# Chunked attention and a feed-forward block on one core: transposes of one pair of token blocks on VectorE, statistics of one tile on ScalarE, and another order of the first tile's steps

## The chip, the core and the metric

The kernel runs on one core of one Trainium2 chip. The metric is the device time of one execution in microseconds. A core has TensorE (PE, with its weight loads shown as PEld), VectorE (DVE), ScalarE (ACT), GpSimd (POOL) and SyncE (SP, which here only issues copies). Each takes its own instructions in program order and waits for others by semaphores.

## The reference, cut to what matters

Attention within chunks of 64 tokens, then a layer norm and a feed-forward block with a residual. There are 8 batches x 576 tokens = 4608 tokens, 8 heads of 64, so 512 features, and 2048 hidden units, all float32.

```python
scores = scale * np.matmul(q_c, k_c.transpose(0, 1, 2, 4, 3))
scores = scores - np.max(scores, axis=-1, keepdims=True)
attn = np.exp(scores)
attn = attn / (np.sum(attn, axis=-1, keepdims=True) + 1e-09)
out = np.matmul(attn, v_c)
...
mu = np.mean(x, axis=-1, keepdims=True)
var = np.mean((x - mu) ** 2, axis=-1, keepdims=True)
xn = (x - mu) / np.sqrt(var + 1e-06) * g_ln
ch = np.maximum(xn @ w_ch1, 0.0) @ w_ch2
return (x + ch).astype(np.float32)
```

## The kernel before, in words

**Tiling.** 256 tokens are a pair, two pairs are a tile of 512 tokens, and there are nine tiles. A tile goes through attention pair by pair and then through the feed-forward block, whose 2048 hidden units are 16 blocks f of 128. Every product of the block is made of three products of rounded numbers: each operand is kept as a high half and a low half (`xth` and `xtl` for the tokens, `hh` and `hl` for the hidden units, two halves in `wp` for the weights), and high x high, high x low and low x high are added up. `up` (L437) makes h of one f, `split` (L447 on ScalarE, L448 on VectorE) rectifies it and splits it into `hh` and `hl`, `down` (L459) adds its share to y. After f = 15, `root` makes 1/sqrt(var + 1e-6), the power on GpSimd (L469), and `finish` (L475) adds the residual.

**Attention of a pair**, as a generator that stops at each `yield`: load q and k; scores into PSUM bank s (L243); maximum `top` (L250) and load of v; subtract it and exponentiate; transpose the probabilities; divide by their sum `den` while the value products (L327) are read out; statistics `mv` by `bn_stats` (L371); the scaled and centred tokens `xg` (L376); their transpose and its split into `xth` and `xtl`. In tile 0 and tile 1 the transposes are done by TensorE (L287, L390), and the low half by a product that subtracts the high half in PSUM (L397, the correction). From tile 2 on VectorE transposes blocks of 32x32 (L298, L410), ScalarE makes the high half (L415) and GpSimd the low half (L416).

**The weights** come as 64-bit floats, and are turned into float32 halves on the chip in 17 units: unit 0 and unit 1 are the two halves of f = 0 (512 KB each), unit i from 2 on is f = i - 1 (1 MB). For each unit SyncE copies it (L105), ScalarE takes the magnitude (L121), VectorE rounds and joins the words (L128, L129, L132) and sets the sign (L139), ScalarE makes the high half (L145). The low half is made by TensorE for units 0 and 1 (L158, L159), for units 2 to 10 by a copy of GpSimd's queue that adds to what ScalarE left there (L147, L162), and for the rest by VectorE (L164).

**The order** of all this is written by hand as strings, one letter for one step of one generator: `START` until tile 0 is through, `STEADY` for each tile in between, `LAST` for the last. a and b are the attention of pairs 0 and 1, A and B that of pairs 2 and 3, E that of the next tile's first pair; w is a step of the weights; u, v, y and 1, 2, 3 are the products and the splits of tile 0 (pair 0 alone, pair 1 alone, both); k is two spare products (L195), whose result nothing reads.

Of the kernel before, what the change touches and what calls it, by code (L numbers as in the profile page):

```python
# [8 lines left out]
F32 = mybir.dt.float32  # L9
# [48 lines left out]
def chunk_attention_ffn(ctx: ExitStack, tc: tile.TileContext, qkv, v01, g, w, out):  # L58
    nc = tc.nc
# [4 lines left out]
    work = ctx.enter_context(tc.tile_pool(name="work", bufs=2))  # L64
# [3 lines left out]
    small = ctx.enter_context(tc.tile_pool(name="small", bufs=4))  # L68
# [134 lines left out]
            ys[pair] = [ps_y.tile([P, DM], F32, name="y") for _ in range(2)]  # L203
        return ys[pair]

    def attention(pair, xt_cols, xs, by_pe, den_by_pe):

        if pair == 1:
            qk = const.tile([P, 2, HP, PAIR], F32, name="qk_b", tag=f"w{NF - 4}")
# [156 lines left out]


        mv = small.tile([P, 2, 2], F32, name="mv", bufs=6)
        for j in range(2):
            stats = small.tile([P, nc.vector.BN_STATS_DIM], F32, name="stats")  # L370
            nc.vector.bn_stats(out=stats, in_=x[:, j, :])  # L371
            nc.vector.bn_aggr(out=mv[:, j, :], in_=stats)
        yield
        xg = work.tile([P, 2, DM], F32, name="xg", tag="work")
        for j in range(2):
            nc.vector.scalar_tensor_tensor(  # L376
                out=xg[:, j, :], in0=x[:, j, :], scalar=mv[:, j, 0:1], in1=g_sb, op0=ALU.subtract, op1=ALU.mult
            )
        yield

        xth, xtl = xt_cols()
        if by_pe:
            xt = halves()
            if den_by_pe:
                taken.add(pair)
            for j in range(2):
                js = slice(j * P, (j + 1) * P)
                for k in range(NK):
                    ks = slice(k * P, (k + 1) * P)
                    nc.tensor.matmul(  # L390
                        xt[j][:, ks], lhsT=xg[:, j, ks], rhs=ident, is_transpose=True, start=k == 0, stop=k == NK - 1
                    )
                nc.scalar.copy(xth[:, :, js], xt[j].rearrange("p (k t) -> p k t", k=NK))
                yield
            for j in range(2):
                js = slice(j * P, (j + 1) * P)
                nc.tensor.matmul(  # L397
                    xt[j], lhsT=minus, rhs=xth[:, :, js], start=False, stop=True, skip_group_check=True
                )
                nc.scalar.copy(xtl[:, :, js], xt[j].rearrange("p (k t) -> p k t", k=NK))  # L400
                if j == 0:
                    yield
            if den_by_pe:
                taken.remove(pair)
        else:
            xt = work.tile([P, 2 * NK, P], F32, name="xt", tag="work")
            xg = xg.rearrange("p j (k t) -> p (j k) t", k=NK)
            for j in range(4):
                for i in range(4):
                    nc.vector.transpose(out=xt[quad(j), :, quad(i)], in_=xg[quad(i), :, quad(j)])  # L410
                yield
            for j in range(2):
                js = slice(j * P, (j + 1) * P)
                xt_j = xt[:, j * NK : (j + 1) * NK, :]
                nc.scalar.copy(xth[:, :, js], xt_j)  # L415
                nc.gpsimd.tensor_tensor(out=xtl[:, :, js], in0=xt_j, in1=xth[:, :, js].bitcast(F32), op=ALU.subtract)  # L416
        xs[pair] = x, mv
        yield

    def ffn(pairs, xt, xs, f0, f1, room=()):  # L420

        nt = len(pairs) * PAIR
        slots = DM // nt
        hs, held = {}, []
        tail = pairs[-1] == 2 * NTILE - 1

        def up(f):
            assert 2 * f in converted and all(pair in xs for pair in pairs)
            h = ps_h.tile([P, nt], F32, name="h")
            xth, xtl = xt()  # L430
            wh, wl = weights(f)
            terms = [(k, m) for k in range(NK) for m in range(3)]
            if f == 0 and nt == PAIR:
                terms.sort(key=lambda t: (0, 2, 1)[t[1]])
            for i, (k, m) in enumerate(terms):
                ks = slice(k * P, (k + 1) * P)
                nc.tensor.matmul(  # L437
                    h, lhsT=(wh, wh, wl)[m][:, ks], rhs=(xth, xtl, xth)[m][:, k, :],
                    start=i == 0, stop=i == len(terms) - 1,
                )  # L440
            hs[f] = h

        def split(f):
            if slots == 1 or not held:
                held[:] = [hp_.tile([P, slots, nt], F32R, name=f"h{i}") for i in "hl"]
            h, (hh, hl) = hs[f], (x[:, f % slots, :] for x in held)
            nc.scalar.activation(hh, h, AF.Relu)  # L447
            nc.vector.scalar_tensor_tensor(  # L448
                out=hl, in0=h, scalar=0.0, in1=hh.bitcast(F32), op0=ALU.max, op1=ALU.subtract
            )  # L450
            hs[f] = hh, hl

        def down(f, j):
            assert 2 * f + 1 in converted
            taken.add(pairs[j // 2])
            hh, hl = (x[:, j * P : (j + 1) * P] for x in hs[f])
            wh, wl = (x[:, DM:] for x in weights(f))
            for m, (hx, wx) in enumerate(((hh, wh), (hh, wl), (hl, wh))):
                nc.tensor.matmul(  # L459
                    sums(pairs[j // 2])[j % 2], lhsT=hx, rhs=wx,  # L460
                    start=f == 0 and m == 0, stop=f == NF - 1 and m == 2,
                )

        def root(pair):
            x, mv = xs[pair]
            vare = small.tile([P, 2], F32, name="vare")
            nc.vector.tensor_scalar_add(vare, mv[:, :, 1], 1e-6)  # L467
            rstd = small.tile([P, 2], F32, name="rstd")
            nc.gpsimd.tensor_tensor(out=rstd, in0=vare, in1=mhalf, op=ALU.pow)  # L469
            xs[pair] = x, rstd  # L470

        def finish(j):
            pair, jj = pairs[j // 2], j % 2
            x, rstd = xs[pair]
            nc.vector.scalar_tensor_tensor(  # L475
                out=x[:, jj, :], in0=sums(pair)[jj], scalar=rstd[:, jj : jj + 1], in1=x[:, jj, :],
                op0=ALU.mult, op1=ALU.add,
            )
            row = pair * PAIR + jj * P
            nc.sync.dma_start(out[row : row + P, :], x[:, jj, :])  # L480

        count = 2 * len(pairs)
        done = []

        def products():
            ups = iter(range(f0, f1))
            for f in range(f0, f1):
                for _ in range((f not in room) + (f == f0 or f - 1 in room or tail and f == NF - 3)):
                    i = next(ups, None)
                    if i is not None:  # L490
# [35 lines left out]
    xs = {}  # L526

    class Tokens:
# [10 lines left out]
        def attention(self, i, by_pe=False, den_by_pe=False):  # L539
            return attention(2 * self.t + i, lambda: self.cols(i), xs, by_pe, den_by_pe)  # L540

        def ffn(self, i, n, f0=0, f1=NF, room=()):
            first = 2 * self.t + i
# [1 line left out]

    tiles = [Tokens(t) for t in range(NTILE)]
    now = {
        "a": tiles[0].attention(0, True, True), "b": tiles[0].attention(1, True, True),
        "A": tiles[1].attention(0, True), "B": tiles[1].attention(1, True),
        "E": tiles[2].attention(0), "w": convert_w(), "k": keep_warm(),  # L550
    }
    now.update(zip("u1", tiles[0].ffn(0, 1, 0, SINGLE)))
# [46 lines left out]
```

## Time and profile before

| | us |
|---|---|
| median of 3 runs | 864.23 (863.54 to 865.45) |
| the profiled execution | 864.05 |
| its span, first to last instruction | 862.3 |

In the profile's rows, a line is a start or a group: the line of the program, engine, operation, what it writes and reads with its shape, and how often it came. The time in brackets behind a row, or behind the second bar of a group, is how long the engine stood idle ahead of it and what ended that. The chain of waits is followed back from the last instruction. Matmul rows overlap, as they are pipelined: the distance from one row's start to the next says what a product takes of the engine.

### The profile page before, as it was taken

To read this page: it belongs to the slowest core of one execution; us is meant where nothing else is said; L and a number is where in the kernel's file an instruction comes from. 1 tells how busy PE (TensorE), PEld (TensorE's weight loads), DVE (VectorE), ACT (ScalarE), POOL (GpSimd) and SP (SyncE) were. 2 spreads that over 40 slices of the span, in tenths; PEclk is the share of its full clock that TensorE was granted. 3 is DMA by queue.
4 is the path that set the end of the run, shared out by engine and by line. 5 is a ranking of instruction groups with operands and counts; after the bars stand their busy time and mean duration, and the time that the engine had idled before them with its cause. 6 is when DMAs were issued, how large, how long until landed. Compare 5 with 4: busy or idle time off the path is not lost.

```text
span 862.3 us, 13752 instructions
## 1 busy us (share of the span) xinstructions
PE 851.6 (99%) x5946; PEld 703.3 (82%) x5946; DVE 526.4 (61%) x960; ACT 178.4 (21%) x267; POOL 56.8 (7%) x64
## 2 busy tenths in 40 slices
PE   7999999999999999999999999999999999999998
PEld 4888888888888888888888888888888888888886
DVE  6999956567656665666667575676566656651112
ACT  5766431121112021201111111211120212011110
POOL 0110000010101010101010100101010101010000
PEclk9999999999999999999999999999999999999999
DMA  9996503200320032001300032003200300010001
GB/s 356 331 302 173 196 0 124 74 1 2 122 74 1 2 120 76 1 1 64 108 25 2 1 122 74 1 2 122 75 1 2 122 26 1 1 49 0 1 1 49
DMA packets 19499, 60.39 MB, mean 70 GB/s; under 512 B 2160, under 2 KB 2160, under 8 KB 17520
## 3 DMA queue, kind: packets, MB, share of 16 engines
q1 hardware_dynamic: 18144, 54.81, 17.6%
q0 software_dynamic: 1296, 4.72, 2.8%
q8 instruction: 46, 0.75, 0.4%
q14 instruction: 13, 0.11, 0.0%
HBM read 45.37 MB, written 9.44 MB: 64 GB/s over the span
## 4 chain that ended last, share of the span: by engine, by line
PE 95%; DVE 3%; DMA 2%; issue 0%; SPq 0%; ACT 0%; DVEq 0%
PE y L459 45%; PE h L437 44%; PE s L243 2%; PE h L327 2%; DMA wp<-wfs 1%; DMA k_t<-qkv 1%; PE s L269 0%; DVE xg L376 0%; DVE wfs L132 0%; DVE stats L371 0%; DVE top L250 0%; DVE wfs L139 0%; PE s L327 0%; PE s L390 0%; DVE wfs L129 0%
## 5 line engine op out<-in xcount | busy, mean ns | idle before, releaser
L437 PE MATMUL h<-xth,wp 128*128 128x512 f32 (+1 forms) x1200 | 377.4, 381 | 0.1
L459 PE MATMUL y<-wp,hh 128*128 128x512 f32 x1152 | 357.0, 391 | 0.0
L448 DVE SCALAR_TENSOR_TENSOR hl<-h,hh 128x512 fp32r<-128x512 f32 (+1 forms) x150 | 100.1, 670 | 280.8 <-ACT hh L447 280.3
L437 PEld LDWEIGHTS h<-xth,wp 128*128 128x128 f32 x1200 | 222.3, 188 | 44.6 <-DVE hl L448 0.8
L459 PEld LDWEIGHTS y<-wp,hh 128*128 128x128 f32 x1152 | 214.3, 188 | 44.5 <-ACT hh L447 0.2
L437 PE MATMUL h<-xtl,wp 128*128 128x512 f32 (+1 forms) x600 | 227.5, 381 | 0.0
L459 PE MATMUL y<-wp,hl 128*128 128x512 f32 x576 | 224.4, 390 | 0.0
L447 ACT ACTIVATE hh<-h 128x512 fp32r<-128x512 f32 (+1 forms) x150 | 86.6, 580 | 562.6 <-PE h L437 543.2
L437 PEld LDWEIGHTS h<-xtl,wp 128*128 128x128 f32 x600 | 112.3, 188 | 21.8 <-ACT xtl L400 0.2
L459 PEld LDWEIGHTS y<-wp,hl 128*128 128x128 f32 x576 | 108.1, 188 | 23.0 <-DVE hl L448 0.4
L410 DVE STREAM_TRANSPOSE xt<-xg 32x256 f32<-32x256 f32 x224 | 97.7, 436 | 3.7
L298 DVE STREAM_TRANSPOSE pt_sb<-p_sb 32x256 f32<-32x256 f32 x224 | 97.6, 436 | 3.1
L416 POOL TENSOR_TENSOR xtl<-xt,xth 128x512 fp32r<-128x512 f32 x28 | 35.6, 1294 | 586.9 <-ACT xth L415 586.9
L475 DVE SCALAR_TENSOR_TENSOR x<-y,rstd,x 128x512 f32<-128x512 f32 x36 | 25.1, 747 | 18.0 <-PE y L459 17.2
L361 DVE TENSOR_TENSOR x<-h,rden 128x512 f32<-128x512 f32 x28 | 18.0, 686 | 12.1 <-PE h L327 12.1
L376 DVE SCALAR_TENSOR_TENSOR xg<-x,mv,g_sb 128x512 f32<-128x512 f32 x36 | 25.3, 744 | 0.0
L371 DVE BATCH_NORM_STATS2 stats<-x 128x6 f32<-128x512 f32 x36 | 24.3, 675 | 0.2
L276 ACT ACTIVATE p_sb<-p_sb 128x1024 f32<-128x1024 f32 x16 | 16.9, 1059 | 35.2 <-DVE p_sb L275 35.2
L250 DVE TENSOR_REDUCE top<-s 128x16 f32<-128x1024 f32 x18 | 21.9, 1216 | 1.5 <-PE s L243 1.5
L415 ACT CAST xth<-xt 128x512 fp32r<-128x512 f32 x28 | 16.0, 618 | 31.5 <-DVE xt L410 31.5
L469 POOL TENSOR_TENSOR rstd<-vare,mhalf 128x2 f32<-128x2 f32 x18 | 12.2, 694 | 141.5 <-DVE vare L467 141.5
L243 PE MATMUL s<-k_t,q_t 64*64 64x64 f32 x1088 | 19.1, 219 | 2.1 <-DMA k_t<-qkv 1.9
(83 smaller groups left out, 308.8 us busy)
## 6 DMA issues: line engine op xcount, KB each, us to landing
raw<-w SPq DMA_DIRECT2D x15, 1024.0 KB, 8.0
out<-x SPq DMA_DIRECT2D x36, 256.0 KB, 2.1
q_t<-qkv SPq DMA_DIRECT2D x17, 512.0 KB, 4.7
k_t<-qkv SPq DMA_DIRECT2D x17, 512.0 KB, 5.7
v_t<-qkv SPq DMA_DIRECT2D x32, 256.0 KB, 4.2
wp<-wfs POOLq DMA_DIRECT2D x6, 512.0 KB, 8.4
wp<-wf POOLq DMA_DIRECT2D x3, 512.0 KB, 6.6
v<-v SPq DMA_DIRECT2D x4, 260.0 KB, 11.0
```

Of the source, the lines that this page charges most:

```text
L243: nc.tensor.matmul(s[h2][c * D : (c + 1) * D, j * HP + a, :], lhsT=q_t[r, a, cs], rhs=k_t[r, a, cs], start=not den_by_pe or j == a == 0, s ...
L250: nc.vector.tensor_reduce(out=top, in_=s4, axis=AX.X, op=ALU.max)
L298: nc.vector.transpose(out=pt_sb[quad(2 * h2 + j), :, c, quad(i)], in_=p_sb[quad(2 * c + i), :, h2, quad(j)])
L371: nc.vector.bn_stats(out=stats, in_=x[:, j, :])
L376: nc.vector.scalar_tensor_tensor(out=xg[:, j, :], in0=x[:, j, :], scalar=mv[:, j, 0:1], in1=g_sb, op0=ALU.subtract, op1=ALU.mult)
L410: nc.vector.transpose(out=xt[quad(j), :, quad(i)], in_=xg[quad(i), :, quad(j)])
L416: nc.gpsimd.tensor_tensor(out=xtl[:, :, js], in0=xt_j, in1=xth[:, :, js].bitcast(F32), op=ALU.subtract)
L437: nc.tensor.matmul(h, lhsT=(wh, wh, wl)[m][:, ks], rhs=(xth, xtl, xth)[m][:, k, :], start=i == 0, stop=i == len(terms) - 1,)
L447: nc.scalar.activation(hh, h, AF.Relu)
L448: nc.vector.scalar_tensor_tensor(out=hl, in0=h, scalar=0.0, in1=hh.bitcast(F32), op0=ALU.max, op1=ALU.subtract)
L459: nc.tensor.matmul(sums(pairs[j // 2])[j % 2], lhsT=hx, rhs=wx, start=f == 0 and m == 0, stop=f == NF - 1 and m == 2,)
L475: nc.vector.scalar_tensor_tensor(out=x[:, jj, :], in0=sums(pair)[jj], scalar=rstd[:, jj : jj + 1], in1=x[:, jj, :], op0=ALU.mult, op1=ALU.add,
```

## The change

Three things change. First, a third flag says who transposes the tokens: pair 3 (B) no longer has it, so its tokens go the way of the later tiles: 16 transposes on VectorE, the high half on ScalarE, the low half on GpSimd. Pair 2 (A) stays with TensorE. Second, in tile 1 (pairs 2 and 3) the mean and the variance no longer come from `bn_stats` but from four sums on ScalarE for each pair: the negative mean from a scaled copy with a summing output, and, behind the transpose, the sum of squares of x minus the mean. `root` divides that sum by 512 in the operation that adds 1e-6. Third, `START` is another string: it has thirteen k in place of fourteen and one B more.

```diff
-START = "kkwkwakwbkwkwkawwwwaawwbwabbkwAkwawbwakkabkkaabaAbabauw1Abbub1Bkbwvuuwuw12wwAvvvw22AwvwvuAvw2wwAvvw1u2AuwwBwvuv12vBuuwyywABA1ww3Ayww3wAywAyuwwwwA3y3BywBBBwBEyyBBwy3w3yywBwwyww3BwwyByy3ywy33yy3E"
+START = "kkwkakwwwwkwwawkkwbawawwAbwbawbkwkwaaabkkbkakaaaAaBbubb1ubwb1uwbbuuwvw1Aw2v2wvAvwv2vwwwvAu2u1AAvwvwuABwu2w1uwvw12ABvwAwuyBwuA3vywwAwy3wAwwy3wwyywwy3AwyByywBBw3wyww3yyB3wwByEywwy3yBwBwyB3ByBE3y3B"
...
+        mean = mv[:, :, 0]
+        act_mean = by_pe and not den_by_pe
+        if act_mean:
+            mean = small.tile([P, 2], F32, name="mean")
+            for j in range(2):
+                square = work.tile([P, DM], F32, name="square", bufs=1)
+                nc.scalar.activation(
+                    square, x[:, j, :], AF.Copy, scale=-1.0 / DM, accum_out=mean[:, j : j + 1]
+                )
-        for j in range(2):
+        for j in range(0 if act_mean else 2):
             stats = small.tile([P, nc.vector.BN_STATS_DIM], F32, name="stats")
...
-                out=xg[:, j, :], in0=x[:, j, :], scalar=mv[:, j, 0:1], in1=g_sb, op0=ALU.subtract, op1=ALU.mult
+                out=xg[:, j, :], in0=x[:, j, :], scalar=mean[:, j : j + 1], in1=g_sb,
+                op0=ALU.add if act_mean else ALU.subtract, op1=ALU.mult,
...
-        if by_pe:
+        if xt_by_pe:
             xt = halves()
...
-        xs[pair] = x, mv
+        if act_mean:
+            for j in range(2):
+                square = work.tile([P, DM], F32, name="square", bufs=1)
+                nc.scalar.activation(
+                    square, x[:, j, :], AF.Square, bias=mean[:, j : j + 1], scale=1.0, accum_out=mv[:, j, 1:2]
+                )
+        xs[pair] = x, mv, 1.0 / DM if act_mean else 1.0
...
-            nc.vector.tensor_scalar_add(vare, mv[:, :, 1], 1e-6)
+            nc.vector.tensor_scalar(
+                out=vare, in0=mv[:, :, 1], scalar1=share, scalar2=1e-6, op0=ALU.mult, op1=ALU.add
+            )
...
-        "A": tiles[1].attention(0, True), "B": tiles[1].attention(1, True),
+        "A": tiles[1].attention(0, True, False, True), "B": tiles[1].attention(1, True),
```

The order moves steps on every engine. At the start of the program SyncE's queue of copies read, before (raw is a unit of the weights, q_t and k_t are of pairs 0 and 2, qk_b of pair 1, v_184 of pair 0 and v_251 of pair 1):

```order
L105 DMA raw<-w 128x512 x2
L215 DMA q_t<-qkv 128x1024
L215 DMA k_t<-qkv 128x1024
L105 DMA raw<-w 128x1024
L215 DMA qk_b<-qkv 128x1024 x2
L105 DMA raw<-w 128x1024
L256 DMA v_184<-v 128x520 x2
L262 DMA g_sb<-g 128x512
L105 DMA raw<-w 128x1024
L256 DMA v_251<-v 128x520 x2
L215 DMA q_t<-qkv 128x1024
L215 DMA k_t<-qkv 128x1024
```

And of the change (v_247 is pair 1's v):

```order
L105 DMA raw<-w 128x512
L215 DMA q_t<-qkv 128x1024
L215 DMA k_t<-qkv 128x1024
L105 DMA raw<-w 128x512
L105 DMA raw<-w 128x1024 x2
L215 DMA qk_b<-qkv 128x1024 x2
L256 DMA v_184<-v 128x520 x2
L262 DMA g_sb<-g 128x512
L105 DMA raw<-w 128x1024
L215 DMA q_t<-qkv 128x1024
L215 DMA k_t<-qkv 128x1024
L256 DMA v_247<-v 128x520 x2
```

Pair 0's q and k moved ahead of unit 1, unit 3 ahead of pair 1's q and k, and pair 2's q and k ahead of pair 1's v.

On ScalarE, from pair 0's exponential to pair 1's transposed probabilities, the rows were:

```order
L273 ACTIVATE p_sb<-s 128x2x8x64
L145 CAST wp<-wfs 128x512
L121 ACTIVATE wf<-raw 128x1024
L160 CAST wp<-y 128x512
L289 COPY pt_sb<-y 128x512 x2
L273 ACTIVATE p_sb<-s 128x2x8x64
L145 CAST wp<-wfs 128x1024
L147 ACTIVATE wp<-wp 128x1024
L121 ACTIVATE wfs<-raw 128x1024
L289 COPY pt_sb<-y 128x512 x2
```

And now they are:

```order
L145 CAST wp<-wfs 128x512
L273 ACTIVATE p_sb<-s 128x2x8x64
L121 ACTIVATE wf<-raw 128x1024
L160 CAST wp<-y 128x512
L145 CAST wp<-wfs 128x1024
L147 ACTIVATE wp<-wp 128x1024
L289 COPY pt_sb<-y 128x512 x2
L273 ACTIVATE p_sb<-s 128x2x8x64
L121 ACTIVATE wfs<-raw 128x1024
L145 CAST wp<-wf 128x1024
L147 ACTIVATE wp<-wp 128x1024
L289 COPY pt_sb<-y 128x512 x2
```

The high half of unit 2 and the copy that starts its low half moved ahead of pair 0's transposed probabilities, and those of unit 3 ahead of pair 1's.

At the end of tile 0 VectorE now has these rows, from the tile's third last rectified product down to its `vare` (the last two units of the weights, L139 and L164, stand among them; before, L385 and L420 were not there, as `xg` of pair 3 came some units sooner and its transposes were TensorE's):

```order
L464 SCALAR_TENSOR_TENSOR hl<-h,hh 128x512
L385 SCALAR_TENSOR_TENSOR xg<-x,mean,g_sb 128x512 x2
L139 SCALAR_TENSOR_TENSOR raw<-raw 128x1024
L420 STREAM_TRANSPOSE xt<-xg 32x8x32 x4
L164 TENSOR_TENSOR wp<-raw,wp 128x1024
L420 STREAM_TRANSPOSE xt<-xg 32x8x32 x4
L464 SCALAR_TENSOR_TENSOR hl<-h,hh 128x512
L420 STREAM_TRANSPOSE xt<-xg 32x8x32 x8
L464 SCALAR_TENSOR_TENSOR hl<-h,hh 128x512
L483 TENSOR_SCALAR vare<-mv 128x2 x2
```

The sixteen transposes of pair 3 thus stand ahead of the rectified products of f = 14 and f = 15.

More of the change, by code (lines that the diff above doesn't have):

```diff
@@ L30 @@
 HALF = NW // 2
-START = "kkwkwakwbkwkwkawwwwaawwbwabbkwAkwawbwakkabkkaabaAbabauw1Abbub1Bkbwvuuwuw12wwAvvvw22AwvwvuAvw2wwAvvw1u2AuwwBwvuv12vBuuwyywABA1ww3Ayww3wAywAyuwwwwA3y3BywBBBwBEyyBBwy3w3yywBwwyww3BwwyByy3ywy33yy3E"
+START = "kkwkakwwwwkwwawkkwbawawwAbwbawbkwkwaaabkkbkakaaaAaBbubb1ubwb1uwbbuuwvw1Aw2v2wvAvwv2vwwwvAu2u1AAvwvwuABwu2w1uwvw12ABvwAwuyBwuA3vywwAwy3wAwwy3wwyywy3AwyByywBBw3wyww3yyB3wwByEywwy3yBwBwyB3ByBE3y3B"
 STEADY = "ABu1Au1AuAu1AuAu1AuABuAu1AEu1AuAu1AuAu1AuAu1BuBu1BuBu1BuBu1BuBEuBBu1BBu1BuBBu1Buu1uu1"
@@ L204, in sums, with attention @@
         return ys[pair]
-    def attention(pair, xt_cols, xs, by_pe, den_by_pe):
+    def attention(pair, xt_cols, xs, by_pe, den_by_pe, xt_by_pe):
         if pair == 1:
@@ L464, in root @@
         def root(pair):
-            x, mv = xs[pair]
+            x, mv, share = xs[pair]
             vare = small.tile([P, 2], F32, name="vare")
-            nc.vector.tensor_scalar_add(vare, mv[:, :, 1], 1e-6)
+            nc.vector.tensor_scalar(
+                out=vare, in0=mv[:, :, 1], scalar1=share, scalar2=1e-6, op0=ALU.mult, op1=ALU.add
+            )
             rstd = small.tile([P, 2], F32, name="rstd")
@@ L537, in cols, with attention @@
             return [x[:, :, i * PAIR : (i + n) * PAIR] for x in self.x]
-        def attention(self, i, by_pe=False, den_by_pe=False):
-            return attention(2 * self.t + i, lambda: self.cols(i), xs, by_pe, den_by_pe)
+        def attention(self, i, by_pe=False, den_by_pe=False, xt_by_pe=False):
+            return attention(2 * self.t + i, lambda: self.cols(i), xs, by_pe, den_by_pe, xt_by_pe)
         def ffn(self, i, n, f0=0, f1=NF, room=()):
@@ L547, in chunk_attention_ffn @@
     now = {
-        "a": tiles[0].attention(0, True, True), "b": tiles[0].attention(1, True, True),
-        "A": tiles[1].attention(0, True), "B": tiles[1].attention(1, True),
+        "a": tiles[0].attention(0, True, True, True), "b": tiles[0].attention(1, True, True, True),
+        "A": tiles[1].attention(0, True, False, True), "B": tiles[1].attention(1, True),
         "E": tiles[2].attention(0), "w": convert_w(), "k": keep_warm(),
```

## The prediction

> **What bounds the kernel now.** I read the page first (busy shares, chain), then the chain of waits in order of time, then the timelines of PE, ACT and DVE in the first 60 us.
>
> ```profile
> PE 851.6 (99%) x5946; PEld 703.3 (82%) x5946; DVE 526.4 (61%) x960; ACT 178.4 (21%) x267; POOL 56.8 (7%) x64
> PE 95%; DVE 3%; DMA 2%; issue 0%; SPq 0%; ACT 0%; DVEq 0%
> ```
>
> TensorE bounds the kernel: it is 95% of the chain, so a saving has to come out of its own work or out of the start, before it runs without a gap. The chain says where that is.
>
> ```profile
> 44.33 8.94 DMA wp<-wfs
> ...
> 53.32 1.45 PE h L437 x10
> ...
> 66.05 1.43 PE h L437 x12
> 67.49 1.39 PE y L459 x6
> ...
> 98.48 0.44 PE s L390 x4
> ...
> 110.32 0.23 PE s L397
> ...
> 124.39 5.44 PE y L459 x24
> 129.83 1.09 PE s L243 x64
> ```
>
> From 53.32 on the chain is TensorE alone, up to the closing rows of the last tile, which the change does not touch. The order of tiles 2 to 8 is not changed either. So the end moves by what the second tile's first product (130.9 us) moves. The waits of TensorE after the first 30 us are almost nothing:
>
> ```profile
> PEld h L437 <- DMA wp<-wfs: 0.3, 1, 0.3
> ```
>
> That one, at 53.3, is for the low half of the fifth weight block (f = 4), brought by an accumulating copy.
>
> **The head.** The rows below are ACT's, DVE's and PE's timelines: start, duration, and in brackets the idle time ahead.
>
> ```profile
> 5.16 0.67 ACT L121 ACTIVATE wf<-raw 128x512 f32<-128x512 f32 x1 [2.82 <-DMA raw<-w]
> 6.42 0.68 ACT L121 ACTIVATE wfs<-raw 128x512 f32<-128x512 f32 x1 [0.59 <-DMA raw<-w]
> 11.46 1.13 ACT L121 ACTIVATE wfs<-raw 128x1024 f32<-128x1024 f32 x1 [2.60 <-DMA raw<-w]
> 13.60 1.02 ACT L273 ACTIVATE p_sb<-s 128x1024 f32<-128x1024 f32 x1 [0.53 <-PE s L269]
> 16.57 1.19 ACT L121 ACTIVATE wf<-raw 128x1024 f32<-128x1024 f32 x1 [1.44 <-DMA raw<-w]
> 19.80 1.03 ACT L273 ACTIVATE p_sb<-s 128x1024 f32<-128x1024 f32 x1 [0.61 <-ACT pt_sb L289]
> 23.77 1.06 ACT L289 COPY pt_sb<-y 128x512 f32<-128x512 f32 x2
> ```
> ```profile
> 5.86 0.43 DVE L128 TENSOR_SCALAR wf<-wf 128x512 f32<-128x512 f32 x1 [5.86 <-ACT wf L121]
> 8.12 0.42 DVE L128 TENSOR_SCALAR wfs<-wfs 128x512 f32<-128x512 f32 x1
> 9.04 0.69 DVE L132 SCALAR_TENSOR_TENSOR wfs<-raw,wfs 128x512 uint32<-128x512 uint32 x1
> 10.30 1.22 DVE L250 TENSOR_REDUCE top<-s 128x16 f32<-128x1024 f32 x1 [0.57 <-PE s L243]
> ```
> ```profile
> 9.08 1.16 PE L243 MATMUL s<-k_t,q_t 64*64 64x64 f32 x64 [1.88 <-DMA k_t<-qkv]
> 14.68 1.16 PE L243 MATMUL s<-qk_b 64*64 64x64 f32 x64 [1.11 <-ACT p_sb L273]
> 17.83 1.88 PE L269 MATMUL s<-top,minus 128*128 128x512 f32 x4
> 20.93 0.70 PE L327 MATMUL s<-v,pt_sb 64*64 64x65 f32 x32 [0.28 <-issue]
> 25.00 0.70 PE L327 MATMUL s<-v,pt_sb 64*64 64x65 f32 x32
> 27.12 1.03 PE L390 MATMUL y<-ident,xg 128*128 128x128 f32 x8
> 30.08 1.11 PE L437 MATMUL h<-xth,wp 128*128 128x256 f32 x8
> ...
> 31.75 1.04 PE L390 MATMUL y<-ident,xg 128*128 128x128 f32 x8
> ```
>
> The copies of SyncE land one behind the other: 512 KB every 1.26 us (5.16 to 6.42), k_t two copies later (9.08), 1 MB in 2.5 (11.46), two halves of qk_b and 1 MB in 5.1 (16.57). The new order issues q_t and k_t ahead of the second weight half and both 1 MB blocks ahead of qk_b. So k_t comes at 7.7, the second half at 9.0, the second half of qk_b at 16.5, not 14.0. From this, step by step:
>
> VectorE still rounds the second half ahead of `top` of pair 0. Its ACT row starts at 9.0; 0.70 later VectorE begins (5.16 to 5.86), 1.61 later it has done L128 to L132 (8.12 to 9.73). `top` starts at 11.3, not 10.30, although its scores are ready by 9.0: 1.0 lost.
>
> The scores of pair 1 start with qk_b at 16.6, not 14.68. Their `top` follows 1.22 later (9.08 to 10.30), at 17.8, and as that takes 1.22, the subtraction of the maxima at 19.0. From there the old distance to pair 0's value products is 3.1 (17.83 to 20.93): 22.1, so 1.2 late, and pair 0's normalised tokens are ready for the transposes at 28.3, not 27.12.
>
> Pair 1's exponential is at 21.0, not 19.80, by its old distance to the maxima (17.83 to 19.80). Behind it ScalarE now has a weight block's L121, L145 and L147 ahead of the copies of pair 1's transposed probabilities (before, L121 alone). L121 waits for the fifth block, which by bytes comes at 21.0 and, as last parts have been landing late, I take at 22.0. Then three operations of 128x1024 at some 1.05 (the rows above have 1.02 to 1.19): copies at 25.1, not 23.77, and pair 1's value products at 26.3, not 25.00. Its v, now behind the next q_t and k_t, comes by bytes at 24.9; the accumulating copy of the second block, issued some 4 us sooner, shares the way, so up to 27.6.
>
> The spare products and pair 0's transposes follow the value products by 2.12, the first useful product the transposes by 2.96. That is 31.4 by the first time and 32.7 by the last; before, 30.08. The old first product ended at 31.75, 1.67 after its start, where one of this size takes 1.43 (66.05); the 0.24 went on the low half of the tokens, whose correction now starts sooner.
>
> So TensorE leaves its first product 1.1 to 2.4 us later; it is nearest to the rows of ScalarE, and with a little for v I take +1.4.
>
> **What goes.** Behind the first product stand, in the same dense run:
>
> ```profile
> 34.29 0.63 PE L195 MATMUL y<-minus 128*128 128x512 f32 x2
> ```
>
> This is the one pair of spare products in it, 128x512 like the one at 110.32, so 0.23 each: -0.46. The other spare products stood, and stand, where TensorE waits. Pair 3's transposes by TensorE (two groups like that at 98.48, 0.44 each) and two corrections (0.23 each, 110.32): -1.34. The old wait at 53.3: -0.3.
>
> **What comes in its place.** The groups:
>
> ```profile
> L410 DVE STREAM_TRANSPOSE xt<-xg 32x256 f32<-32x256 f32 x224 | 97.7, 436 | 3.7
> L416 POOL TENSOR_TENSOR xtl<-xt,xth 128x512 fp32r<-128x512 f32 x28 | 35.6, 1294 | 586.9 <-ACT xth L415 586.9
> L371 DVE BATCH_NORM_STATS2 stats<-x 128x6 f32<-128x512 f32 x36 | 24.3, 675 | 0.2
> L400 ACT CAST xtl<-s 128x512 fp32r<-128x512 f32 x4 | 2.3, 585 | 0.0
> ```
> ```profile
> 119.68 0.69 DVE L448 SCALAR_TENSOR_TENSOR hl<-h,hh 128x512 fp32r<-128x512 f32 x1 [0.23 <-ACT hh L447]
> 125.06 0.69 DVE L448 SCALAR_TENSOR_TENSOR hl<-h,hh 128x512 fp32r<-128x512 f32 x1 [4.69 <-ACT hh L447]
> ```
>
> VectorE gets 16 transposes, 16 x 0.436 = 7.0, and loses four statistics, 2.7 (and their aggregation). They stand among the tile's last weight blocks and its last three rectified products, where it was idle 4.69 ahead of the last one alone and TensorE leaves 5.44 from one product to the next; eight of them (3.5) fit into the last gap. Cost nothing; without the cover, up to 3.5. The order puts GpSimd's two subtractions (2.6) behind both `rstd`, which follow the last rectified product. Counting from that product's end: 0.67 to hl, 0.6 to vare, 0.3 and two `rstd` of 0.7, then 2.6 make 5.6; TensorE needs the low half after down(14), the scores and down(15), 2.7 + 1.1 + 2.7 = 6.5. Nothing, with 0.9 to spare.
>
> ScalarE's eight new operations (mean, then variance) no row shows. The nearest is a copy of 128x512, 0.585; the summing on top is unknown, so 0.6 to 1.1 each. The mean stands ahead of `xg`, with `top` of pair 3 (1.2) running on VectorE meanwhile; pair 3's variances have a whole product to hide behind. The new share in `vare` is a scalar in an operation that was there. Nothing, at worst 1.0.
>
> The weights are the open part:
>
> ```profile
> 40.58 1.22 DVE L139 SCALAR_TENSOR_TENSOR wfs<-raw,wfs 128x1024 uint32<-128x1024 uint32 x1
> ```
> ```profile
> DMA to landing us min/median/max: 4.6/8.2/9.6
> ```
> ```profile
> 40.00:50.00 10.00, 10.00 (x71) 9.27 (x70) 9.83 (x15) 8.69 (x12) 1.63 (x2) 1.00 1.04 299
> ```
>
> The sign step of block f = 4 (40.58) now stands behind the rectified second product of pair 1. From 33.1, the end of the first product (31.75 + 1.4), TensorE does four products of 1.45, two down of 1.39, transposes and corrections (1.3) and up(1) again 1.45: it ends at 42.9 or so; ACT and DVE add 0.8, so 43.7, 3.1 late. The old way from there to the issue was 3.75 (44.33): 47.4, landing at 52.0 to 57.0, 55.6 by the median. TensorE reaches it after four down, three up, the transposed probabilities and value products, 4 x 1.39 + 3 x 1.45 + 0.9 + 1.1, at 55.0. So a wait of 0 to 2.0, by the median +0.6.
>
> **Sum**, against the profiled execution's 864.05 (span 862.3 and 1.75 around it; the median of three runs is 864.23, so it is an ordinary run): 864.05 + 1.4 - 0.46 - 1.34 - 0.3 + 0.6 = 863.95, told as 863.9. What is taken away is real, and the head gives it back.
>
> On sharing, the Trainium skill, "DMA: Bandwidth & Descriptors", section "Queues, rings and completion order", says that each engine takes one queue's entries in ring order and goes round between queues by packets. The equal steps of SyncE's copies agree with the first half. By the second half the accumulating copy of GpSimd takes turns with v, the upper end of the head, and the sum would be 864.9.
>
> **The rivals.**
>
> The head is not late (20%, faster). If the copies issued within 2 us share the engines, the second weight half lands with k_t and `top` starts when the scores end; qk_b would not be held back either. Then only the removals stand: 864.05 - 0.46 - 1.34 - 0.3 = 861.95. The steps of 1.26 us speak against it.
>
> The DMA engines are full (14%, slower). Their share is 1.04 at 40 to 50 us. If the earlier accumulating copy holds v to 27.6, the head costs 2.4; and if f = 4 takes 9.6 from its issue, its wait is 2.0: 864.05 + 2.4 - 2.1 + 2.0 = 866.35. It decides from the point at which v lands after 25.2 and the copy takes over 7.6. Eight microseconds is the median, which speaks for it; that the fullness eases as blocks start later speaks against it.
>
> The change does not do its part in the second tile (4%): VectorE comes late to the transposes, and GpSimd's low half is not there at the first product of tile 1. From 0.9 late on each microsecond is lost; with one it is 864.9.
>
> The forecast has the other 62%.
>
> About 0.2% (1.7 us) is what a measurement of this kernel can tell from no change. Below 862.5 lies the first rival, above 866.0 the second; the third and the forecast lie between: faster 0.20, same 0.66, slower 0.14. The range reaches to the two rivals, 861.8 to 866.3; it holds both ends of the unknown costs.
>
> **What would show it.** In the new trace: pair 0's `top` at 11.3 with VectorE idle ahead of it for ScalarE; scores of pair 1 at 16.6 behind a DMA; the first product at 31.4 to 32.7; a wait for the copy of f = 4 near 55 of up to 2.0; no wait of TensorE at tile 1's first product, which should start near 130.8. A first product at or before 30.1 would make me wrong to the fast side, waits for weight copies of over 2 us in all to the slow side.

## The result, and the profile after

The changed kernel takes 869.99 us in the median (868.64 to 871.03, six runs), the kernel before beside it 864.9 (863.54 to 865.45, six runs): a ratio of 1.0059, interval 1.0045 to 1.0072. It is slower by 0.6%, outside the predicted range and on the other side of the forecast. The profiled execution took 870.59, with a span of 868.5; that is 6.5 more than the profiled 864.05 of before.

First the page of the changed kernel, the busy times and the shares of the chain:

```profile
PE 851.8 (98%) x5934; PEld 703.4 (81%) x5934; DVE 531.0 (61%) x968; ACT 183.1 (21%) x281; POOL 59.4 (7%) x66
PE 92%; DMA 4%; DVE 3%; POOL 0%; SPq 0%; issue 0%; ACT 0%; POOLq 0%; ACTq 0%
```

TensorE has twelve instructions less and is busy as long as before, and its share of the chain went from 95% to 92%. So it lost time in waits, and something made its instructions longer. Both are seen in its timeline (start, duration, tile, count, idle time ahead):

```profile
25.29 1.19 PE L195 MATMUL y<-minus 128*128 128x512 f32 x4 [0.74 <-DVE x L347]
28.87 0.70 PE L327 MATMUL s<-v,pt_sb 64*64 64x65 f32 x32 [2.38 <-POOL v L280]
29.38 0.90 PE L327 MATMUL y<-v,pt_sb 64*64 64x65 f32 x32
30.21 2.07 PE L195 MATMUL y<-minus 128*128 128x512 f32 x4
32.09 1.50 PE L400 MATMUL y<-ident,xg 128*128 128x128 f32 x8
...
35.67 1.12 PE L453 MATMUL h<-xth,wp 128*128 128x256 f32 x8
```

Pair 1's value products start at 28.87, not 25.00, behind a wait of 2.38 for v. The four spare products after them take 2.07 where four such products took 1.19 ahead of the wait, and the first useful product starts at 35.67, where it was 30.08 (`up` is L453 now, a pair's transposes L400, `hl` L464). The table by windows says why; the columns behind the engines' busy times are the granted clock, the share of the DMA engines, and GB/s:

```profile
28.00:32.00 4.00, 3.13 (x68) 2.61 (x69) 2.24 (x8) 0.00 (x0) 0.99 (x2) 0.70 0.64 170
32.00:36.00 4.00, 3.77 (x78) 3.09 (x77) 3.16 (x7) 1.79 (x4) 0.00 (x0) 0.87 0.33 62
```

The clock was 0.70 and 0.87 there, 1.00 in all such windows of before from 8 to 72 us. That is 4 x 0.30 + 4 x 0.13 = 1.7 us of TensorE's pulses; in a window from 29.60 to 33.01 us alone the clock reads 0.50. It was no accident of the profiled execution: the mean clock over the span is 0.997 or 0.998 in all six executions. GpSimd's timeline shows when v came, as its memset writes the ones into v:

```profile
18.06 0.13 POOL L280 MEMSET v<- 128x16 f32 x1 [16.75 <-DMA v<-v]
19.47 1.15 POOL L162 DMA_DIRECT2D wp<-wfs  x1 [1.27 <-DVE top L250]
28.69 0.12 POOL L280 MEMSET v<- 128x16 f32 x1 [8.07 <-DMA v<-v]
```

The accumulating copy of the second weight block is issued at 19.47 (23.19 before), and pair 1's v is there at 28.6. Further on TensorE has these waits from 20 to 140 us, in total, times and longest:

```profile
PE s L327 <- POOL v L280: 2.4, 1, 2.4
PE h L453 <- DMA wp<-wfs: 1.7, 2, 1.0
PE h L453 <- POOL xtl L426: 1.1, 1, 1.1
```

The second row is two weight blocks' low halves (f = 3 and f = 4, 0.63 and 1.03). The third stands at tile 1's first product, where I had foreseen no wait. VectorE, ScalarE and GpSimd ahead of it:

```profile
128.17 0.69 DVE L464 SCALAR_TENSOR_TENSOR hl<-h,hh 128x512 fp32r<-128x512 f32 x1
128.90 3.60 DVE L420 STREAM_TRANSPOSE xt<-xg 32x256 f32<-32x256 f32 x8
132.52 0.69 DVE L464 SCALAR_TENSOR_TENSOR hl<-h,hh 128x512 fp32r<-128x512 f32 x1
133.13 0.23 DVE L483 TENSOR_SCALAR vare<-mv 128x2 f32<-128x2 f32 x2
```
```profile
129.33 0.60 ACT L463 ACTIVATE hh<-h 128x512 fp32r<-128x512 f32 x1 [4.30 <-PE h L453]
```
```profile
133.44 1.38 POOL L487 TENSOR_TENSOR rstd<-vare,mhalf 128x2 f32<-128x2 f32 x2 [48.43 <-DVE vare L483]
134.79 2.52 POOL L426 TENSOR_TENSOR xtl<-xt,xth 128x512 fp32r<-128x512 f32 x2
```

The last rectified product was ready for VectorE at 129.9 and was taken at 132.52, behind eight transposes without a gap. `rstd` waits for it, and pair 3's low half stands behind `rstd` in GpSimd's queue and ends at 137.3; TensorE stood there from 136.2.

The account by the traces: first product +5.6, less 0.2 that it no longer spends on the tokens' low half (1.44 from its start to its end, where it was 1.67), waits for low halves of weights +1.66 - 0.3, wait for GpSimd +1.14, less 0.46 of spare products and 1.34 of transposes: +6.1. The first `down` of tile 1 starts 6.28 later (136.59 and 142.87), so 0.2 is left over; the span is longer by 6.2.

### The profile page after: what moved, and what is told of

Its sections match the earlier page's. It is cut to its first block, busy times and chain, and to the rows that moved or that the text cites. A ratio compares the mean times of both kernels' runs of the same rounds, so it can differ in the third digit from the quotient of the medians.

```text
span 868.5 us, 13746 instructions
## 1 busy us (share of the span) xinstructions
PE 851.8 (98%) x5934; PEld 703.4 (81%) x5934; DVE 531.0 (61%) x968; ACT 183.1 (21%) x281; POOL 59.4 (7%) x66
## 4 chain that ended last, share of the span: by engine, by line
PE 92%; DMA 4%; DVE 3%; POOL 0%; SPq 0%; issue 0%; ACT 0%; POOLq 0%; ACTq 0%
PE h L453 44%; PE y L475 43%; PE h L327 2%; PE s L243 2%; DMA qk_b<-qkv 1%; DMA v<-v 1%; DMA wp<-wfs 1%; DVE xt L420 1%; DVE wp L164 0%; DVE hl L464 0%; POOL xtl L426 0%; DVE raw L139 0%; SPq L105 0%; PE y L195 0%; PE s L327 0%
## 5 line engine op out<-in xcount | busy, mean ns | idle before, releaser
L453 PE MATMUL h<-xth,wp 128*128 128x512 f32 (+1 forms) x1200 | 377.0, 381 | 1.7 <-DMA wp<-wfs 1.7
L464 DVE SCALAR_TENSOR_TENSOR hl<-h,hh 128x512 fp32r<-128x512 f32 (+1 forms) x150 | 100.4, 670 | 280.2 <-ACT hh L463 279.6
L453 PEld LDWEIGHTS h<-xth,wp 128*128 128x128 f32 x1200 | 222.5, 188 | 45.4 <-DMA wp<-wfs 2.1
L453 PE MATMUL h<-xtl,wp 128*128 128x512 f32 (+1 forms) x600 | 227.4, 381 | 1.1 <-POOL xtl L426 1.1
L453 PEld LDWEIGHTS h<-xtl,wp 128*128 128x128 f32 x600 | 112.4, 188 | 23.3 <-POOL xtl L426 1.6
L420 DVE STREAM_TRANSPOSE xt<-xg 32x256 f32<-32x256 f32 x240 | 104.7, 436 | 4.0
L426 POOL TENSOR_TENSOR xtl<-xt,xth 128x512 fp32r<-128x512 f32 x30 | 38.1, 1292 | 583.3 <-ACT xth L425 583.3
L385 DVE SCALAR_TENSOR_TENSOR xg<-x,mv,g_sb 128x512 f32<-128x512 f32 x32 | 22.5, 744 | 0.0
L380 DVE BATCH_NORM_STATS2 stats<-x 128x6 f32<-128x512 f32 x32 | 21.6, 675 | 0.2
```

What stands on the lines that cost most here:

```text
L385: nc.vector.scalar_tensor_tensor(out=xg[:, j, :], in0=x[:, j, :], scalar=mean[:, j : j + 1], in1=g_sb, op0=ALU.add if act_mean else ALU.su ...
L453: nc.tensor.matmul(h, lhsT=(wh, wh, wl)[m][:, ks], rhs=(xth, xtl, xth)[m][:, k, :], start=i == 0, stop=i == len(terms) - 1,)
L464: nc.vector.scalar_tensor_tensor(out=hl, in0=h, scalar=0.0, in1=hh.bitcast(F32), op0=ALU.max, op1=ALU.subtract)
```

## The experiments

The theory after the result, H: the head costs nearly all, because v of pair 1 comes late and TensorE's clock falls in the wait; the end of tile 0 costs 1.1 by GpSimd's queue; the removed work is saved as predicted. The rival E: the two edits themselves (transposes on VectorE, statistics on ScalarE) cost, whatever the order.

Each ratio is to runs of the kernel before on the same chip. The median of these is 864.9 beside the changed kernel and 864.25 to 864.7 beside the others, so the difference of two rows comes out up to 1 us smaller by the ratios than by the medians.

| kernel | median us | ratio to before, interval |
|---|---|---|
| changed kernel | 869.99 | 1.0059 (1.0045 to 1.0072) |
| v ahead | 866.44 | 1.0030 (1.0015 to 1.0046) |
| edits in the old order | 871.16 | 1.0080 (1.0065 to 1.0095) |
| new order alone | 872.76 | 1.0098 (1.0083 to 1.0113) |
| rstd early | 867.74 | 1.0041 (1.0026 to 1.0056) |
| v ahead and rstd early | 864.87 | 1.0002 (0.9992 to 1.0012) |
| statistics alone | 867.88 | 1.0044 (1.0029 to 1.0059) |
| transposes alone | 868.59 | 1.0049 (1.0034 to 1.0064) |
| spare products ahead | 867.39 | 1.0033 (1.0021 to 1.0046) |
| accumulating copy behind v | 865.63 | 1.0013 (1.0003 to 1.0022) |
| shorter head | 866.40 | 1.0021 (1.0011 to 1.0030) |
| shorter head, xg off VectorE | 866.40 | 1.0025 (1.0015 to 1.0034) |
| copy behind v and rstd early | 864.28 | 1.0002 (0.9992 to 1.0011) |

**v ahead.** In `START`, the first A (load of pair 2's q and k) goes behind b's third step:

```diff
-...wawwAbwbawbk...
+...wawwbwbAawbk...
```

> The changed kernel, with pair 1's v (and the maximum beside it) ahead of the load of pair 2's q and k; nothing else moves. Theory H (the head: v of pair 1 comes late, TensorE waits for it and its clock falls): v lands some 2.5 us sooner, at 26.1 in place of 28.57, the value products of pair 1 start at 26.3 to 26.8, the spare products behind them cost 0.23 each and not 0.43, the first useful product starts near 32, and the total falls by 3 to 4 us, to about 866.5. Rival W (the weight blocks set the pace): the first product is as early, but the waits for the low halves of f = 3 and f = 4 grow by as much, total 868.5 to 870. Rival S (it is the spare products and not v): the first product stays after 34.

GpSimd's memset of v, and TensorE's value products and first useful product:

```profile
23.72 0.12 POOL L280 MEMSET v<- 128x16 f32 x1 [3.15 <-DMA v<-v]
```
```profile
26.36 0.70 PE L327 MATMUL s<-v,pt_sb 64*64 64x65 f32 x32
...
31.62 1.12 PE L453 MATMUL h<-xth,wp 128*128 128x256 f32 x8
```

v came 5 us sooner, more than the 2.5 of the two copies that went behind it. The lateness went over to the last of these two: pair 2's k lands at 28.26 now, by the trace's semaphore events, and is needed only for scores at 30.19. There is no wait for v and no fall of the clock (the four spare products take 1.19 again), the first product stands at 31.62, and the total fell by 3.5 (2.6 by the ratios). H holds, S falls. The waits for low halves stayed at 1.5 and did not grow as W had it.

**Edits in the old order.** `START` as before with one B more (`...wwyByy3Bywy33yy3E`); everything else as changed.

> The changed kernel's new transposes and statistics, with the order of before and one B more, ahead of the last rectified products. Theory H: the order costs all of it, and the two other edits pay what I gave them: first product at 30.1, one tile's transposes and corrections by TensorE less, no wait at tile 1's first product; 864.9 - 1.3 = 863.6. Rival E (the edits themselves cost, VectorE's eight transposes ahead of the last rectified product): TensorE waits at the end of tile 0 by 1 us or more, total 864.9 or above.

871.16: the head is that of before (first product at 30.27), and still it is as slow as the changed kernel, or slower. The wait of TensorE, then ScalarE and VectorE ahead of it:

```profile
PE y L475 <- DVE hl L464: 3.8, 2, 3.6
```
```profile
97.23 1.12 ACT L121 ACTIVATE wf<-raw 128x1024 f32<-128x1024 f32 x1 [5.81 <-DMA raw<-w]
98.25 1.09 ACT L145 CAST wp<-raw 128x1024 fp32r<-128x1024 f32 x1
99.25 0.63 ACT L375 ACTIVATE square<-x 128x512 f32<-128x512 f32 x1
```
```profile
100.00 1.51 DVE L385 SCALAR_TENSOR_TENSOR xg<-x,mean,g_sb 128x512 f32<-128x512 f32 x2 [3.34 <-ACT square L375]
101.55 1.78 DVE L420 STREAM_TRANSPOSE xt<-xg 32x256 f32<-32x256 f32 x4
...
105.94 0.68 DVE L464 SCALAR_TENSOR_TENSOR hl<-h,hh 128x512 fp32r<-128x512 f32 x1
```

The mean of pair 3 stands behind a weight block that ScalarE waits for; VectorE idles 3.34 for it, and the rectified product stands behind `xg`, four transposes and a rounding. The clock falls here too: in a window from 106.47 to 109.88 us, from just before the end of that wait of 3.6 on, it reads 0.50, another 1.7 us, and the mean clock is 0.996 to 0.998 in all four executions. H, that the order costs all of it, falls: in the old order the edits cost 0.8%.

**New order alone.** The kernel before with the new `START`, less its last B.

> The kernel before with the new order and nothing else: pair 3's tokens transposed by TensorE, statistics on VectorE, one B less. Theory H: the first product as late as in the changed kernel, 35.7, and the waits for f = 3 and f = 4 as there; 1.3 more of TensorE's work and no wait of 1.1 for GpSimd's low half, so about 870.2. Rival E: without the new transposes it is 868.5 or less.

872.76, more than either theory. The head is as H has it: pair 1's value products start at 28.86 behind a wait of 2.45, the clock reads 0.50 from 28.39 to 31.81 us, and the first product stands at 35.43. What H lacked are waits later on. TensorE waits where pair 3's transposes by TensorE now stand close behind one another, with ScalarE's copies between them:

```profile
PE s L397 <- ACT xth L393: 0.7, 1, 0.7
...
PE s L243 <- ACT xtl L400: 0.7, 1, 0.7
```

So order and edits can't be priced apart: alone the order costs 1.0% and the edits 0.8%, together 0.6%, and each of the three holds a fall of the clock.

**rstd early.** `root` goes with the split of f = 14:

```diff
-                if f == NF - 1:
+                if f == NF - 2:
```

> The changed kernel with the power on GpSimd (rstd) one block sooner in every tile, with the split of f = 14, so that GpSimd's subtractions for pair 3's low half stand no longer behind it. If GpSimd's queue makes the wait of 1.1 us at tile 1's first product: the low half is there at 135.7 in place of 137.3, the wait goes, total 868.9. If VectorE's transposes set it (they end at 132.5, and the last rectified product behind them): the wait shrinks by less than 0.3 and the total stays at 870.

The wait at tile 1's first product is gone. The total fell by 2.25 by the medians and by 1.6 by the ratios, whose intervals are over 1 us wide to each side, so this is not clearly more than the 1.1 expected. In this profiled run the two waits for low halves of weights are absent too, with the head as late as in the changed kernel (first product at 35.73). For f = 4 that is the copy's own time: it was issued at 51.74 here and at 51.67 in the changed kernel, and landed at 56.86 here and at 61.26 there. How often each happens is not known, as one trace is kept of each kernel.

**v ahead and rstd early,** both edits.

> The changed kernel with both of the edits that helped: pair 1's v ahead of pair 2's q and k, and rstd one block sooner. If the two losses are separate and add: 866.4 less 1.1 (the wait for GpSimd's low half that is still in the run with v ahead), 865.3; if the waits for the low halves of f = 3 and f = 4 go too, as in the run with rstd sooner, 863.8. Rival: with the head sooner another engine (VectorE at the end of tile 0, ScalarE's waits for weight blocks near 90 us) takes the place, total 866 or more.

864.87: within the noise the two gains add, and the change is back at the time of before. In the profiled run (863.41, the fastest of the ten) no wait of TensorE is left between 40 and 140 us. `rstd` is now made ahead of the transposes' end:

```profile
123.15 1.38 POOL L487 TENSOR_TENSOR rstd<-vare,mhalf 128x2 f32<-128x2 f32 x2 [44.09 <-DVE vare L483]
127.42 2.56 POOL L426 TENSOR_TENSOR xtl<-xt,xth 128x512 fp32r<-128x512 f32 x2 [2.90 <-ACT xth L425]
```

**Statistics alone,** in the order of before, with pair 3 transposed by TensorE:

```diff
-        "A": tiles[1].attention(0, True, False, True), "B": tiles[1].attention(1, True),
+        "A": tiles[1].attention(0, True, False, True), "B": tiles[1].attention(1, True, False, True),
```

> The kernel before with nothing but tile 1's mean and variance on ScalarE; pair 3 stays with TensorE, order of before. If the sums on ScalarE cost nothing, as I put it: 864.2. Rival Q (they stand in ScalarE's queue behind a weight block): pair 3's mean stands behind the L121 that waits near 95.5 us for a weight block, so xg comes some 2.5 us later than at 96.76, TensorE waits 1.4 to 2.4 us for it at pair 3's transposes near 98.5: 865.7 to 866.7.

867.88, 3.2 more than before and worse than Q. TensorE's new waits are three: at pair 3's transposes for `xg`, as Q has it, though smaller (1.0), and two at rectified products, which come late from VectorE and ScalarE:

```profile
PE h L453 <- DVE hl L464: 1.0, 1, 1.0
PE s L400 <- DVE xg L385: 1.0, 1, 1.0
...
PE y L475 <- ACT hh L463: 0.7, 1, 0.7
```

**Transposes alone,** in the order of before with one B more, `bn_stats` kept:

```diff
-        act_mean = by_pe and not den_by_pe
+        act_mean = False
```

> The kernel before with nothing but pair 3's tokens by VectorE and GpSimd (and the one B more that this needs); statistics on VectorE, order of before. If VectorE has room between the last weight blocks: 864.25 - 1.3 = 863.0. Rival D (its steps stand in VectorE's queue ahead of the rounding of weight blocks and of rectified products): the wait of 3.6 us that the run with the old order has near 103 us stays, by 2 us or more, total 866 or above.

868.59, so rival D holds. VectorE, four transposes and what stands behind them:

```profile
98.47 1.78 DVE L420 STREAM_TRANSPOSE xt<-xg 32x256 f32<-32x256 f32 x4
...
102.88 0.68 DVE L464 SCALAR_TENSOR_TENSOR hl<-h,hh 128x512 fp32r<-128x512 f32 x1
```

Before, that rectified product was taken at 100.65; TensorE waits 1.75 for it, and in shorter pieces later on. Its first product of tile 1 is 4.2 later (135.04, where it was 130.85), with 1.34 less of its own work.

**Spare products ahead.** The changed kernel with two k moved ahead of pair 1's value products:

```diff
-...aaabkkbkakaaaAaB...
+...aaabkkkkbaaaaAaB...
```

> The changed kernel with four spare products moved ahead of pair 1's value products; v comes as late as before (28.6). TensorE then idles 1.2 us less ahead of v, and has four products less behind it. Theory C (the clock falls by TensorE's idling): with an idle time of some 1.3 us in place of 2.4 the products behind cost 0.23 and not 0.43, the first useful product starts at 32.7, total 867. Rival C2 (the clock falls all the same): first product at 33.7, total 868. Rival W: the weight blocks' waits take it back, 869 or more.

The value products and the first useful product, and the first window again:

```profile
28.91 0.70 PE L327 MATMUL s<-v,pt_sb 64*64 64x65 f32 x32 [1.55 <-POOL v L280]
...
33.20 1.12 PE L453 MATMUL h<-xth,wp 128*128 128x256 f32 x8
```
```profile
28.00:32.00 4.00, 2.85 (x87) 2.30 (x91) 2.41 (x8) 1.20 (x3) 0.98 (x2) 1.00 0.63 171
```

v is as late, TensorE idles 1.55 in place of 2.38, and the clock stays at 1.00. The first product is 2.47 sooner: 0.9 for four products that no longer stand behind v, the rest is the clock. The mean clock is 0.999 or 1.000 in all six executions, where the changed kernel has 0.997 or 0.998. This is theory C; the total of 867.39 is near its 867.

**Accumulating copy behind v.** The order of SyncE's copies stays; GpSimd's memset moves to the load of v, ahead of that copy in GpSimd's queue:

```diff
+            nc.gpsimd.memset(v_1.rearrange("p j a b d -> p (j a b) d")[:, :, D:], 1.0)
             yield
...
-        if den_by_pe:
-            nc.gpsimd.memset(v_1.rearrange("p j a b d -> p (j a b) d")[:, :, D:], 1.0)
```

> The changed kernel with one thing moved: GpSimd's memset of the ones in pair 1's v stands ahead of the accumulating copy of the second weight block in GpSimd's queue. The memset waits for v, so that copy is issued only when v is there, not at 19.5; the order of SyncE's copies stays. It tells what made v land at 28.6 when its bytes were due at 24.9. Theory P (the accumulating copy took turns with v): v lands between 24.5 and 26, the value products of pair 1 start at 26.5, the clock stays, the first useful product starts near 32, total 866 to 867. Rival I (v waits for something else, such as one slow DMA engine): v still lands after 27.5 and the total stays at 869 to 870. Either way the low half of f = 1 lands later by some 4 us, which could add a wait at its first product.

GpSimd, then TensorE (the lines are two lower here):

```profile
26.35 0.13 POOL L257 MEMSET v<- 128x16 f32 x1 [8.16 <-DMA v<-v]
26.93 1.05 POOL L162 DMA_DIRECT2D wp<-wfs  x1 [0.45 <-ACT pt_sb L287]
```
```profile
26.54 0.70 PE L325 MATMUL s<-v,pt_sb 64*64 64x65 f32 x32
...
31.79 1.12 PE L451 MATMUL h<-xth,wp 128*128 128x256 f32 x8
```

v lands at 26.25, not 28.58, with the same copies ahead of it: 2.3 of its lateness is the accumulating copy that ran beside it. The clock stays (a mean of 0.999 or 1.000 in all ten executions), the first product is at 31.79, the total 865.63. This is theory P. The later low half of f = 1 cost no wait.

**Shorter head,** and **shorter head with xg off VectorE.** Both start from v ahead and rstd early. The scores of pair 2 go behind the first two products, and four spare products are left out; the second also makes pair 3's `xg` by ScalarE and GpSimd.

```diff
-...bkkbkakaaaAaBbubb1ub...
+...bkkbaaaaaBbubb1uAb...
```

> The run with v ahead and rstd sooner (864.9), with the scores of pair 2 moved behind the first two products and the four spare products behind pair 1's value products left out. The first product then starts at 30.0 in place of 31.65. If TensorE is what bounds the rest of tile 0: 864.9 - 1.6 = 863.2. Rival V (VectorE's steps from 97 to 127 us, with the low halves of the last blocks 0.1 to 0.6 ahead of their products, are as tight): what the head gains turns into waits there, 864.3 to 864.9.

> As the run before it in this list, with pair 3's scaled tokens made by ScalarE (subtract the mean) and GpSimd (times g) and not by VectorE: 1.3 us less in VectorE's queue ahead of the last weight block, 1.2 more in ScalarE's ahead of a rectified product. If VectorE's end of tile 0 eats the gain of the head (rival V), this one is faster than the head alone by 0.4 or more; if TensorE bounds, the two agree within 0.3.

Both 866.40, slower than what they start from. The first product did come sooner (30.25), but neither theory has the place where it was lost; TensorE's waits, and ScalarE ahead of the second:

```profile
PE h L453 <- DMA wp<-wfs: 1.4, 1, 1.4
PE y L475 <- ACT hh L463: 1.2, 1, 1.2
```
```profile
42.63 1.12 ACT L121 ACTIVATE wf<-raw 128x1024 f32<-128x1024 f32 x1 [1.99 <-DMA raw<-w]
43.65 0.65 ACT L463 ACTIVATE hh<-h 128x256 fp32r<-128x256 f32 x2
```

ScalarE waits for a weight block with the rectified product queued behind it. TensorE came 1.4 sooner to a place where the weights were not. Nothing of rival V could show, as the gain never got to 97 us.

**Copy behind v and rstd early,** the two edits on GpSimd's queue together, the new order untouched.

> The changed kernel, its order untouched, with two edits on GpSimd's queue alone: the memset of pair 1's ones ahead of the accumulating copy of the second weight block, and rstd one block sooner. If the loss against the kernel before is these two places of GpSimd's queue, it goes: 865.6 less 1.1, so 864.5, the time of before. Rival: a loss that has nothing to do with them stays (the late head of 1.5 us, waits for low halves of weight blocks), 865.2 or more.

864.28. With two places in GpSimd's queue mended the whole loss against the kernel before is gone. No version that was tried beats the kernel before.

## Why the prediction was wrong, point by point

**The head, +1.4 (1.1 to 2.4): wrong; it was 5.6 at the start of the first product, and 5.4 at its end, from which the term counts.** The steps up to pair 1's scores came as told: `top` of pair 0 at 11.28, scores of pair 1 at 16.72, pair 0's value products at 22.36 (told: 22.1). The step that failed is "Its v ... comes by bytes at 24.9; the accumulating copy ... shares the way, so up to 27.6", from which I took little. v came at 28.6. The mechanism stood there and in the second rival; its size was off by 1.0 at the upper end, and I chose the lower. The run with the copy behind v shows it: 26.3 without that neighbour. By the Trainium skill, "DMA: Bandwidth & Descriptors", section "Queues, rings and completion order", a DMA engine goes round between its queues by packets. The two landings agree with queues that share; no run here shows in what portions.

The second failed step is "The spare products and pair 0's transposes follow the value products by 2.12, the first useful product the transposes by 2.96". From 28.87 that gives 33.95; it was 35.67. The missing 1.7 is the clock, which I had not counted at all. A late v made TensorE idle, and that made the next 3.4 us slow; the run with spare products ahead takes the wait below 1.6 and the clock stays. Once v comes on time the head is 1.5 to 1.7 late (31.62, 31.79), which is what the rest of that term (1.4) had said.

**The removed work, -0.46 - 1.34 - 0.3: it agrees, though it was not tried by itself.** With the two places of GpSimd's queue mended, the kernel before (864.41 in those runs), the head's 1.7 and these -2.1 give 864.0; measured were 864.28. The profiled run, at 865.94 one of the slowest of the ten, has waits for low halves of 1.5 in it.

**The weights, +0.6 (0 to 2.0): right in kind, on the low side.** The copy of f = 4 was issued at 51.67, not 47.4, as the head was 4 us later than told; it took 9.59 to land, the upper end that I had given it, and cost 1.03. f = 3, for which I had no wait, cost 0.63. In the run with `rstd` early both are absent, so which size comes out is partly luck. The working names "up(1) again 1.45" as one more product, but its 42.9 holds four products of 1.45 in all; the trace has four there, so the sum stands and the list was wrong.

**Pair 3's low half, "Nothing, with 0.9 to spare": wrong, 1.14.** The step that failed is "eight of them (3.5) fit into the last gap". The gap of 4.69 was one of the old order. Nor do all sixteen transposes stand ahead of the rectified product of f = 14: eight do, and the other eight stand between it and that of f = 15. In the new run VectorE ends the rectified product of f = 14 at 128.86, 0.5 before ScalarE begins on that of f = 15 (129.33), so the eight transposes between them push the latter back by about 2.6. I counted 5.6 from the last product to the low half; from 129.07, where the product ended, it was 8.25 (137.32). The run with `rstd` early takes GpSimd's queue out of that path, and the wait is gone.

**ScalarE's sums, "Nothing, at worst 1.0": right here, not in general.** An operation takes 0.63 to 0.72 with 0.19 to read the sum, within my 0.6 to 1.1, and no wait of TensorE in the changed kernel points to them. In the old order they cost 3.2 alone; one of TensorE's three waits there comes from pair 3's mean, which stands behind a weight block's row in ScalarE's queue. So "nothing" was a property of the new order, which I had not worked out.

**The rivals.** The first (the head not late) is out. The second had the right place and the right resource but ended at 866.35, as it lacked the clock. The third (pair 3's low half late, with 4% of the chance) came true, at 1.14 where it had put 1 us; the true end is the second and third together and the clock. The range left out that they could come at once.

## What to carry to other kernels

A transfer that comes late is priced with what TensorE's clock does in the wait, not with the wait alone; where it can't be made sooner, work ahead of the wait keeps the clock. A copy that is issued sooner on one queue takes bandwidth from what is due next on another (2.3 us here), so look at each neighbour of a moved copy, not only at its own landing. A gap of an engine in the old trace is no room for new work unless the new order still has it there: count again from when that engine ends the instruction ahead.

## What the runs showed of the hardware

The clock fell after less idleness than I would have thought. TensorE stood 2.38 us, with 0.74 idle shortly before and 1.2 busy between; the clock then read 0.50 from 29.60 to 33.01, which is the loss of 1.7 us of pulses. It fell alike in two other kernels, late in a wait of 2.45 (new order alone) and late in one of 3.6 (edits in the old order). With 1.55 of idle time in place of the 2.38 it did not fall. The Trainium skill, "TensorE: Matmul & The Clock Gate", section "What's actually happening", has half the clock after at least one idle window of about 3.4 us. The length and the half agree with the trace (0.50 for 3.41 us). But here it took no whole window of idleness: in the 3.4 us ahead of the fall TensorE was busy for 1.03.

A copy's sixteen parts did not land together where the DMA engines were full (a share of 1.05 from 24 to 28 us in the changed kernel). These are the landings of the second half of pair 1's v (us from the start, by the trace's semaphore events), in the changed kernel and with the copy behind v:

```
24.13 24.19 24.22 24.24 24.27 24.32 24.33 24.66 24.96 24.99 25.37 25.49 25.82 25.98 26.71 28.58
24.17 24.18 24.25 24.36 24.36 24.37 24.43 24.51 24.58 24.63 24.66 24.67 24.74 24.81 24.98 26.25
```

Eight parts and more were in by 24.7 in both, near my time by bytes (24.9). Beside the accumulating copy the others come later, and in both cases the last part is 1.3 to 1.9 behind the fifteenth. The same shows at f = 4's copy: its fifteenth part landed at 56.52 in the changed kernel and at 56.60 with `rstd` early, its last at 61.26 and at 56.86, so the wait for it was for one part of sixteen. What holds that one back was not tried and stays open.
